# Lane numbering, the stored T and two split transfers in a recurrent-attention and expert kernel

## The chip, the cores and the metric

One core of one Trainium2 chip runs the whole program. The metric is device time in microseconds (us), of one execution of the program. Several executions of the kernel before were timed, and one was profiled.

## The reference, cut to what matters

All inputs are fp32 except the two dense weight matrices, which arrive as 64-bit floats and are converted on the chip. A recurrence over 768 steps runs for 4 batches of 8 heads with 40 x 40 states; its output, as 3072 tokens of 320 features, goes through a dense two-layer block (ELU between) and then through eight experts, chosen per token.

```python
# r, k, v, w, a, b: [4, 8, 768, 40]
for t in range(768):
    y[:, :, t] = einsum('bhd,bhde->bhe', rt, state)
    Sa = einsum('bhde,bhe->bhd', state, at)
    state = state * wt[:, :, None, :] - einsum('bhd,bhe->bhde', Sa, bt) + einsum('bhd,bhe->bhde', vt, kt)
x = y as [3072, 320]
h = x @ w_in                                   # [320, 2048]
x = where(h > 0, h, exp(min(h, 0)) - 1) @ w_out  # [2048, 320]
probs = softmax(x @ w_gate); e = argmax        # 8 experts
out[i] = probs[e] * (relu(x[i] @ w1[e]) @ w2[e])   # w1: 320 x 1024, w2: 1024 x 320
```

## The kernel before, in words

The 768 steps are cut into 24 chunks of 32 steps (C = 32). Two chunks make a pair (12 pairs), four chunks make a lane group (6 groups). There are 32 (batch, head) combinations.

**Lanes.** `lanes(g)` works on one group: 128 partitions, one for each of 4 chunks times 32 heads, each holding 32 steps x 40 features (1280 floats, 5 KB). It loads w, forms running products along the steps, multiplies a by them and stores the result to DRAM (`scr_A`), stores the products (`scr_W`), loads w again, forms the inverse products from the other end, multiplies b and k by those and stores both (`scr_BK`). Group 0 (the call with `room`) has its four loads and its stores on SP's DMA queue and its own tiles; groups 1 to 5 have five loads and four stores each on POOL's queue, in two tiles (`W`, `lx`) that are used again and again, and their arithmetic on POOL, in order with what else POOL does. Three places of a group wait on a load: L161 for w, L185 for the second w, L196 for k.

**Pairs.** `pre(p)` reads the scaled a, b, k by steps (`load_tok`: `tok` tiles, steps on partitions, 160-byte pieces), transposes them, multiplies, and masks the result into `TM`, whose T part goes to DRAM (`Td`, L290, two transfers per chunk). `inverse(p)` reads T back with one lane per partition (L306, twice, 64 lanes each), inverts 64 unit triangular 32 x 32 matrices on DVE by 31 rounds of about three instructions (L314, L319, L321), writes the result to DRAM (`Ud`, L325) and reads it back for each chunk as `UT` (L328). `chain(c)` is the recurrence proper for one chunk: products with `TM`, `UT` and the state `ST`, an evacuation times `Wp` at L448 near its end, and the loads of the next chunk's `Wp`, `BKd` and `pv`. `put` transposes the finished chunk for the dense block.

**Around it.** While the first chunks run, `Moe1.weights` converts the dense weights in 40 steps: a load on SP's queue into one of three `raw` buffers (L495), ACT (L499), DVE (L500 to L503), ACT (L472), and for the low part POOL (L473, L510). `Moe1.block(p)` is the dense block on the two chunks of pair p, `Router.tile(c)` then ranks the experts for one chunk, stores its 128 rows of 321 floats to DRAM (`rows`, L699, one transfer on SP) and scatters the token numbers (`list`). Then `Moe2` gathers rows by expert and runs the eight experts.

Generators are woven by step counts (`weave`), with priorities from `ahead`; the order of each engine's queue is then made by a planner that plays the program through with costs of its own (`schedule_with_timeline_sim=True`). Each engine and SP's queue run their instructions in that order, and an instruction that waits holds up all behind it on its engine.

```python
weave((ahead(tc, start(), 1000), 100), (conv, 60))   # start: lanes(0), pre(0), lanes(1), inverse(0), pre(1)
for p in range(NP + 1):
    ... chain(2p), chain(2p+1); lanes(p//2 + 2) over two p; inverse(p+1); pre(p+2); moe1.block(p-1)
```

Of the kernel before, what the change touches and what calls it, by code (L numbers as in the profile page):

```python
# [22 lines left out]
B, H, S, D = 4, 8, 768, 40  # L23
C = 32
NCH = S // C
NP = NCH // 2
# [7 lines left out]
ROW = DM + 1  # L34
# [4 lines left out]
class Attention:  # L39
# [7 lines left out]
    def __init__(self, ctx, tc, nc, r, k, v, w, a, b):  # L47
        self.nc, self.tc = nc, tc
        self.src = dict(r=r, k=k, v=v, w=w, a=a, b=b)

        def pool(name, **kw):
            return ctx.enter_context(tc.tile_pool(name=name, bufs=1, **kw))

        self.pers = pool("att", side="right")
        self.dr = pool("att_dram", space=DRAM)
        dr = lambda shape, name: self.dr.tile(shape, F32, name=name)
        self.scr_A = [dr([128, C, D], f"scr_A{g}") for g in range(NP // 2)]
        self.scr_W = [dr([128, C, D], f"scr_W{g}") for g in range(NP // 2)]
        self.scr_BK = [dr([128, 2 * C, D], f"scr_BK{g}") for g in range(NP // 2)]
        self.Td = [dr([C, 64, C], f"Td{p}") for p in range(NP)]  # L60
        self.Ud = [dr([C, 64, C], f"Ud{p}") for p in range(NP)]
        self.tiles = {}

# [62 lines left out]
    def lanes(self, g, eng, eng2=None, room=None):  # L126

        nc = self.nc
        eng2 = eng2 or eng
        W, la, wd = self.t("W"), self.t("lx"), self.t("WCd")
        V, lb, lk = room or (W, la, la)
        flat = lambda t: t.rearrange("p s d -> p (s d)")
        queue = nc.sync if room else nc.gpsimd

        def load(t, x):
            queue.dma_start(
                flat(t), self.src[x][:, :, 128 * g:128 * g + 128, :].rearrange("b h (c s) d -> c (b h) (s d)", c=4))  # L140

        def store(dst, t):
            for i in (0, 64) if room else (0,):
                q = slice(i, i + 64) if room else slice(0, 128)
                self.last = queue.dma_start(dst[q], t[q])

        w = V[:, 0:32, :] if room else W[:, 1:33, :]
        load(w, "w")
        load(la, "a")
        if room:  # L150
            load(lb, "b")
            load(lk, "k")
        nc.vector.memset(W[:, 0, :], 1.0)
        yield

        eight = lambda t: t.rearrange("p (q r) d -> p q r d", r=8)
        wq, Wq = eight(w), eight(W[:, 1:33, :])
        if room:
            eng.tensor_copy(Wq[:, :, 0], wq[:, :, 0])
        for r in range(1, 8):  # L160
            eng.tensor_tensor(Wq[:, :, r], Wq[:, :, r - 1], wq[:, :, r], ALU.mult)  # L161
            yield
        for q in range(1, 4):
            eng.tensor_tensor(
                Wq[:, q], Wq[:, q], W[:, 8 * q, :].unsqueeze(1).to_broadcast([128, 8, 40]), ALU.mult)
            yield
        nc.vector.tensor_copy(wd[:, 0:40], W[:, 32, :])
        nc.vector.tensor_copy(wd[:, 64:104], W[:, 32, :])
        nc.gpsimd.tensor_tensor(la, la, W[:, 0:32, :], ALU.mult)
        store(self.scr_A[g], la)  # L170
        if not room:
            store(self.scr_W[g], W[:, 0:32, :])
            load(W[:, 0:32, :], "w")
            load(lb, "b")
        ps = self.psum("p")
        nc.tensor.transpose(ps[0:104, 0:128], wd, self.ident)
        wt = self.t("WCT", g)
        v = ps[:, 0:128].rearrange("p (c i j) -> p c i j", c=4, j=2)
        nc.vector.tensor_copy(wt[0:40], v[0:40, :, :, 0])
        nc.vector.tensor_copy(wt[64:104], v[64:104, :, :, 1])  # L180
        yield
        nc.vector.reciprocal(V[:, 32, :], wd[:, 0:40])
        Vq = eight(V[:, 0:32, :])
        for r in range(6, -1, -1):
            eng.tensor_tensor(Vq[:, :, r], Vq[:, :, r + 1], Vq[:, :, r], ALU.mult)  # L185
            yield
        for q in range(3, -1, -1):
            eng.tensor_tensor(
                Vq[:, q], Vq[:, q], V[:, 8 * q + 8, :].unsqueeze(1).to_broadcast([128, 8, 40]), ALU.mult)
            yield  # L190
        eng2.tensor_tensor(lb, lb, V[:, 1:33, :], ALU.mult)
        store(self.scr_BK[g][:, 0:C], lb)
        if not room:
            load(lk, "k")
        yield
        nc.gpsimd.tensor_tensor(lk, lk, V[:, 1:33, :], ALU.mult)  # L196
        store(self.scr_BK[g][:, C:2 * C], lk)
        if room:
            for _ in range(2):
                self.load_tok()  # L200
            yield
            with self.tc.issue_after(self.last.ins):
                store(self.scr_W[g], W[:, 0:32, :])
        yield

    def load_heads(self, t, src, hg, s0, n):

        self.nc.sync.dma_start(
            t[:, :, 0:40], src[2 * hg:2 * hg + 2, :, s0:s0 + n, :].rearrange("b h s d -> s (b h) d"))

    def load_tok(self):

        if self.loaded == len(self.order):
            return
        kind, i = self.order[self.loaded]
        t = self.t("tok", self.loaded)
        self.loaded += 1
        for hg in range(2):
            rows = t[64 * hg:64 * hg + 64]
            if kind == "r":  # L220
                self.load_heads(rows, self.src["r"], hg, 64 * i, 64)
            elif kind == "a":
                for cc in range(2):
                    lane = (2 * (i % 2) + cc) * 32 + 16 * hg
                    self.nc.sync.dma_start(
                        rows[32 * cc:32 * cc + 32, :, 0:40],
                        self.scr_A[i // 2][lane:lane + 16].rearrange("l s d -> s l d"))
            else:
                lane = (i % 4) * 32 + 16 * hg
                self.last = self.nc.sync.dma_start(  # L230
                    rows[:, :, 0:40], self.scr_BK[i // 4][lane:lane + 16].rearrange("l x d -> x l d"))

    def turn(self, tag, evac):
        t = self.t("tok", self.taken)
# [25 lines left out]
    def pre(self, p):  # L260

        nc = self.nc
# [11 lines left out]
        for cc in range(2):  # L274
            c = 2 * p + cc
            ps = self.psum("p")
# [7 lines left out]
            TM = self.t("TM", c)  # L284
# [3 lines left out]
            )  # L288
            for hg in range(2):
                self.last = self.nc.sync.dma_start(  # L290
                    self.Td[p][:, 32 * cc + 16 * hg:32 * cc + 16 * hg + 16, :].rearrange("s l t -> s (l t)"),
                    TM[64 * hg:64 * hg + 32, :])
            if cc == 0:
                self.block_diagonal(Abd, AAT, 1, 'ss')
                yield
# [3 lines left out]
    def inverse(self, p):  # L299

        nc = self.nc
        TL, UL = self.t("TL"), self.t("UL")
        nc.vector.memset(UL, 0.0)
        for i in range(2):
            half = slice(64 * i, 64 * i + 64)
            self.last = self.nc.sync.dma_start(TL[half], self.Td[p].rearrange("s l t -> l s t"))  # L306
            nc.vector.memset(UL[half].rearrange("p a b -> p (a b)")[:, i::34], 1.0)
        yield
        for j in range(31):

            n, m = j // 2 + 1, 30 - j
# [13 lines left out]
            self.nc.sync.dma_start(  # L325
                self.Ud[p].rearrange("(a i) l t -> i l a t", i=2)[i], UL[64 * i:64 * i + 64])
        for cc in range(2):
            self.nc.sync.dma_start(  # L328
                self.t("UT", 2 * p + cc).rearrange("p h t -> p (h t)"),
                self.Ud[p][:, 32 * cc:32 * cc + 32, :].rearrange("s (b h) t -> b s (h t)", b=4))  # L330
        yield

    def load_pv(self, c):
# [2 lines left out]

    def load_bkd(self, c):
        for hg in range(2):
            lane = (c % 4) * 32 + 16 * hg
            self.nc.sync.dma_start(  # L340
                self.t("BKd", c)[64 * hg:64 * hg + 64], self.scr_BK[c // 4][lane:lane + 16].rearrange("l x d -> x l d"))

    def load_wp(self, c):
        for b in range(4):
            lane = (c % 4) * 32 + 8 * b
            self.nc.sync.dma_start(
                self.t("Wp")[32 * b:32 * b + 32].rearrange("p (h d) -> p h d", h=8),
                self.scr_W[c // 4][lane:lane + 8].rearrange("h s d -> s h d"))

    def bank(self, c):  # L350

# [265 lines left out]
class Router:  # L617
# [52 lines left out]
    def tile(self, c, o):  # L670
        nc, p = self.nc, self.p
        x2 = self.new_x2()
# [4 lines left out]
        s = lambda n, dt=F32, w=1: p.tile([128, w], dt, tag=n, name=n, bufs=1)  # L677
# [10 lines left out]
        ps = o[:, 400:512]  # L688
# [4 lines left out]
        at, place = s("at", w=E), s("place")  # L693
# [2 lines left out]
        nc.vector.tensor_reduce(place, at, AX.X, ALU.add)  # L696
        idx = p.tile([128, 1], I32, tag="idx", name="idx", bufs=2)
        self.last = nc.vector.tensor_copy(idx, place)  # L698
        nc.sync.dma_start(self.rows.rearrange("(b s) d -> b s d", b=B)[:, C * c:C * c + C, :], x2[:, 0:ROW])  # L699
        nc.gpsimd.indirect_dma_start(  # L700
            out=self.list[:, :], out_offset=bass.IndirectOffsetOnAxis(ap=idx.bitcast(U32)[:, 0:1], axis=0),
            in_=self.ids[:, c:c + 1], in_offset=None, bounds_check=E * LIST - 1, oob_is_err=False,
# [497 lines left out]
```

## Time and profile before

| what | value |
|---|---|
| timed runs of the kernel before | 1306.5, 1322.2, 1322.34 us; median 1322.2 us |
| the profiled execution | 1325.83 us |
| its span, first to last instruction | 1324.0 us, granted TensorE clock 0.927 of full |
| busy share of the span | PE 78%, DVE 61%, ACT 45%, POOL 23% |
| DMA | 325,645 packets, 131.27 MB, of which 292,808 packets are under 512 B |

The span is cut into 40 slices on the page; PE's busy share is low in the first ten and near 9 tenths from there on, while the DMA engines' mean busy share is highest in the first half. A mean over 16 DMA engines does not tell whether all of them are busy.

### The profile page before, as it was taken

Reading aid. Unit: us, or ns where it says so; the run is one execution under the profiler, and the core shown is the slowest. Engines: PE = TensorE matmul, PEld = TensorE weight load, DVE = VectorE, ACT = ScalarE, POOL = GpSimd, SP = SyncE. Lnnn points to the kernel's source line nnn. Section 1 sums busy time; section 2 is a strip of 40 time slices with the busy share of each in tenths; the row PEclk is TensorE's granted clock in tenths of the full one; section 3 lists DMA queues with packets and bytes.
Section 4 is the critical chain, followed back from the end, with each engine's and each line's share of the span. In section 5 each row is a group of like instructions: output and inputs, shape, how many; then the busy total and the mean of one; then the engine's idle time right before and its main releaser. Section 6 shows DMA issues by size and latency. Waiting matters only on the chain.

```text
span 1324.0 us, 35742 instructions
## 1 busy us (share of the span) xinstructions
PE 1037.8 (78%) x14568; PEld 945.8 (71%) x14568; DVE 802.2 (61%) x2714; ACT 598.3 (45%) x1498; POOL 299.6 (23%) x355
## 2 busy tenths in 40 slices
PE   0144165777769988989899999989989679999994
PEld 0133155666668777878788888889989679889994
DVE  2345675677448864878667686867555425655541
ACT  0233123445425544546455655656656425534430
POOL 4343253454231341021000000000000141232311
PEclk9999996898779988899899999989999879999997
DMA  3767456655563566455452536342130146545210
GB/s 99 167 157 134 114 128 135 139 154 107 134 141 68 112 125 132 68 100 104 68 88 45 90 56 101 53 81 49 28 89 11 35 116 174 138 127 162 76 41 19
DMA packets 325645, 131.27 MB, mean 99 GB/s; under 512 B 292808, under 2 KB 307280, under 8 KB 325472
## 3 DMA queue, kind: packets, MB, share of 16 engines
q1 hardware_dynamic: 304848, 89.24, 34.4%
q0 software_dynamic: 19664, 37.43, 10.1%
q8 instruction: 117, 1.92, 0.7%
q10 hardware_dynamic: 960, 2.23, 0.6%
q14 instruction: 56, 0.46, 0.1%
HBM read 99.13 MB, written 31.00 MB: 98 GB/s over the span
## 4 chain that ended last, share of the span: by engine, by line
DMA 27%; PE 24%; DVE 23%; issue 11%; ACT 3%; POOL 3%; SPq 2%; another core or an unknown queue 0%; ACTq 0%; POOLq 0%; DVEq 0%
DMA W<-in_w_dram 5%; PE ps_h L583 4%; DMA out_dram<-ys,ids 4%; DVE ut L314 3%; DVE inv L319 3%; DMA inv<-Td 3%; DVE inv L321 3%; PE ps_c L375 3%; DMA lx<-in_k_dram 2%; DMA raw<-in_moe_w_in_dram 2%; DMA Ud<-inv 2%; DVE ST L421 2%; PE ps_c L903 2%; PE ps_h L903 2%; DVE e L589 2%
## 5 line engine op out<-in xcount | busy, mean ns | idle before, releaser
L472 ACT CAST gH<-e 128x256 fp32r<-128x256 f32 x192 | 77.0, 405 | 136.0 <-DVE e L589 128.4
L597 PE MATMUL ps_o<-woH,gH 128*128 128x328 f32 x384 | 130.2, 341 | 9.6 <-ACT gH L472 9.6
L599 PE MATMUL ps_o<-woH,gL 128*128 128x328 f32 x384 | 120.7, 336 | 8.3 <-DVE gL L473 8.2
L598 PE MATMUL ps_o<-woL,gH 128*128 128x328 f32 x384 | 126.0, 330 | 0.0
L583 PE MATMUL ps_h<-xH,wiH 128*128 128x256 f32 x368 | 112.5, 307 | 13.4 <-DVE e L589 12.6
L700 POOL DMA_INDIRECT list<-ids,idx x24 | 24.6, 1026 | 429.9 <-DVE idx L698 322.0
L589 DVE SCALAR_TENSOR_TENSOR e<-e,ps_h 128x256 f32<-128x256 f32 x184 | 76.5, 417 | 60.5 <-ACT e L588 58.2
L314 DVE TENSOR_TENSOR ut<-inv 128x30 f32<-128x30 f32 (+4 forms) x360 | 95.1, 264 | 26.9 <-DMA inv<-Td 26.5
L583 PE MATMUL ps_h<-xL,wiH 128*128 128x256 f32 x368 | 109.7, 298 | 0.0
L583 PE MATMUL ps_h<-xH,wiL 128*128 128x256 f32 x368 | 109.0, 296 | 0.0
L473 DVE TENSOR_TENSOR gL<-e,gH 128x256 fp32r<-128x256 f32 x192 | 81.5, 429 | 30.2 <-ACT gH L472 26.8
L319 DVE SCALAR_TENSOR_TENSOR inv<-inv 128x1 f32<-128x1 f32 (+15 forms) x372 | 98.1, 264 | 0.5
L321 DVE TENSOR_TENSOR inv<-inv,ut 128x30 f32<-128x30 f32 (+4 forms) x360 | 96.0, 267 | 0.3
L587 ACT ACTIVATE e<-ps_h 128x256 f32<-128x256 f32 x184 | 70.7, 384 | 54.4 <-PE ps_h L583 35.2
L244 PE MATMUL ps_p<-ident,tok 128*104 128x128 f32 x288 | 55.5, 321 | 41.0 <-DMA tok<-scr_A 15.4
L583 PEld LDWEIGHTS ps_h<-xH,wiH 128*128 128x128 f32 x368 | 73.7, 201 | 18.7 <-DVE e L589 17.6
L597 PEld LDWEIGHTS ps_o<-woH,gH 128*128 128x128 f32 x384 | 77.6, 202 | 12.0 <-ACT gH L472 10.7
L599 PEld LDWEIGHTS ps_o<-woH,gL 128*128 128x128 f32 x384 | 73.8, 200 | 10.7 <-DVE gL L473 9.7
L588 ACT ACTIVATE e<-e 128x256 f32<-128x256 f32 x192 | 79.1, 416 | 4.1
L598 PEld LDWEIGHTS ps_o<-woL,gH 128*128 128x128 f32 x384 | 77.8, 203 | 0.2
L583 PEld LDWEIGHTS ps_h<-xL,wiH 128*128 128x128 f32 x368 | 74.6, 203 | 0.1
L583 PEld LDWEIGHTS ps_h<-xH,wiL 128*128 128x128 f32 x368 | 74.2, 202 | 0.0
(308 smaller groups left out, 2882.4 us busy)
## 6 DMA issues: line engine op xcount, KB each, us to landing
r<-in_moe_w_dram SPq DMA_DIRECT2D x15, 640.0 KB
tok<-scr_BK SPq DMA_DIRECT2D x48, 160.0 KB
BKd<-scr_BK SPq DMA_DIRECT2D x48, 160.0 KB
r<-in_moe_w_dram SPq DMA_DIRECT2D x7, 1024.0 KB
W<-in_w_dram POOLq DMA_DIRECT2D x10, 640.0 KB
scr_BK<-lx POOLq DMA_DIRECT2D x10, 640.0 KB
inv<-Td SPq DMA_DIRECT2D x24, 256.0 KB
raw<-in_moe_w_out_dram SPq DMA_DIRECT2D x16, 320.0 KB
```

Of the source, the lines that this page charges most:

```text
L314: nc.vector.tensor_tensor(tv, TL[:, j:j + 1, j + 2:32].to_broadcast([128, n, m]), UL[:, 0:n, j:j + 1].to_broadcast([128, n, m]), ALU.mult,)
L319: nc.vector.scalar_tensor_tensor(col, UL[:, 0:n, j], TL[:, j, j + 1:j + 2], col, ALU.mult, ALU.add)
L321: nc.vector.tensor_tensor(UL[:, 0:n, j + 2:32], UL[:, 0:n, j + 2:32], tv, ALU.add)
L472: split.last = nc.scalar.copy(H, x)
L473: return (low or nc.vector).tensor_tensor(L, x, H.bitcast(F32), ALU.subtract)
L583: nc.tensor.matmul(h, l, r, start=i == 0, stop=i == len(seq) - 1)
L587: nc.scalar.activation(e, h, AF.Relu, scale=-1.0)
L588: nc.scalar.activation(e, e, AF.Exp, scale=-1.0)
L589: nc.vector.scalar_tensor_tensor(e, e, -1.0, h, ALU.add, ALU.max)
L597: nc.tensor.matmul(o, gH[:, ts], self.woH[:, f], start=f == 0, stop=False)
L598: nc.tensor.matmul(o, gH[:, ts], self.woL[:, f], start=False, stop=False)
L599: nc.tensor.matmul(o, gL[:, ts], self.woH[:, f], start=False, stop=f == NF - 1)
```

## The change

Lanes are numbered head first: partition 4 x head + chunk instead of 32 x chunk + head. The load of L140 therefore lists the 32 heads before the 4 chunks on its DRAM side; the bytes are the same, 128 pieces of 5 KB. The DRAM copies of the lanes have the same order, and `of` picks the lanes of one chunk with a stride of four in the loads of `tok`, `BKd` and `Wp`, whose pieces stay as long as they were. The copy out of PSUM into `WCT` reads with a stride. T is stored lane by lane, `[64, 32, 32]`: its store now writes 32 x 16 pieces of 128 bytes in place of 32 pieces of 2 KB, and each of its two loads reads 64 pieces of 4 KB in place of 64 x 32 pieces of 128 bytes. The load of `UT` for a chunk becomes four transfers of 32 partitions (one per batch) in place of one whose outermost dimension is 4, and so does the store of `rows`.

```diff
-        self.Td = [dr([C, 64, C], f"Td{p}") for p in range(NP)]
+        self.Td = [dr([64, C, C], f"Td{p}") for p in range(NP)]
...
-                flat(t), self.src[x][:, :, 128 * g:128 * g + 128, :].rearrange("b h (c s) d -> c (b h) (s d)", c=4))
+                flat(t), self.src[x][:, :, 128 * g:128 * g + 128, :].rearrange("b h (c s) d -> (b h) c (s d)", c=4))
...
-        v = ps[:, 0:128].rearrange("p (c i j) -> p c i j", c=4, j=2)
+        v = ps[:, 0:128].rearrange("p (i j c) -> p c i j", c=4, j=2)
...
+    def of(self, t, c, first, n):
+
+        return t.rearrange("(l c) s d -> c l s d", c=4)[c, first:first + n]
...
-                    rows[:, :, 0:40], self.scr_BK[i // 4][lane:lane + 16].rearrange("l x d -> x l d"))
+                    rows[:, :, 0:40], self.of(self.scr_BK[i // 4], i % 4, 16 * hg, 16).rearrange("l x d -> x l d"))
...
-                    self.Td[p][:, 32 * cc + 16 * hg:32 * cc + 16 * hg + 16, :].rearrange("s l t -> s (l t)"),
-                    TM[64 * hg:64 * hg + 32, :])
+                    self.Td[p][32 * cc + 16 * hg:32 * cc + 16 * hg + 16].rearrange("l s t -> s l t"),
+                    TM[64 * hg:64 * hg + 32, :].rearrange("s (l t) -> s l t", t=C))
...
-            self.last = self.nc.sync.dma_start(TL[half], self.Td[p].rearrange("s l t -> l s t"))
+            self.last = self.nc.sync.dma_start(TL[half], self.Td[p])
...
         for cc in range(2):
-            self.nc.sync.dma_start(
-                self.t("UT", 2 * p + cc).rearrange("p h t -> p (h t)"),
-                self.Ud[p][:, 32 * cc:32 * cc + 32, :].rearrange("s (b h) t -> b s (h t)", b=4))
+            for b in range(4):
+                h = 32 * cc + 8 * b
+                self.returned = self.nc.sync.dma_start(
+                    self.t("UT", 2 * p + cc)[32 * b:32 * b + 32], self.Ud[p][:, h:h + 8, :])
...
-        nc.sync.dma_start(self.rows.rearrange("(b s) d -> b s d", b=B)[:, C * c:C * c + C, :], x2[:, 0:ROW])
+        for b in range(B):
+            at = S * b + C * c
+            nc.sync.dma_start(self.rows[at:at + C, :], x2[C * b:C * b + C, 0:ROW])
```

The loads of `tok` from `scr_A`, of `BKd` and of `Wp` take their lanes through `of` in the same way.

## Rows read from the trace of the kernel before

**Rows 1.** Busy time by engine in two stretches: clock, DMA share, GB/s last

```profile
core 0: us, PE busy (x) PEld busy (x) DVE busy (x) ACT busy (x) POOL busy (x), PEclk, DMA share, GB/s
0.00:400.00 400.00, 205.38 (x2954) 180.50 (x2954) 227.21 (x704) 131.15 (x343) 159.56 (x214) 0.89 0.60 134
400.00:971.00 571.00, 526.46 (x9781) 478.23 (x9776) 407.67 (x1584) 323.65 (x853) 58.69 (x61) 0.95 0.45 79
```

**Rows 2.** L448, once per chunk: ns min/median/max, first and last start

```profile
L448 DVE TENSOR_TENSOR xtok<-ps_c,Wp x5: 475/478/491, 200.6 to 398.7; 128x320 f32<-128x320 f32 x5
...
L448 DVE TENSOR_TENSOR xtok<-ps_c,Wp x18: 427/482/492, 200.6 to 970.7; 128x320 f32<-128x320 f32 x18
```

**Rows 3.** Chain of waits that ended last, 0 to 400 us, shares by line

```profile
by line: DMA W<-in_w_dram 15.6%; DMA lx<-in_k_dram 7.0%; DMA raw<-in_moe_w_in_dram 7.0%; DMA raw<-in_moe_w_out_dram 4.5%; issue 3.9%; DMA Ud<-inv 2.7%; DMA inv<-Td 2.6%; POOL W L161 2.6%; DVE ut L314 2.4%; DVE x L502 2.4%; SPq L230 2.0%; DV
```

**Rows 4.** Who waited for whom, 0 to 400 us: total us, times, longest

```profile
DVE x L500 <- ACT x L499: 75.1, 20, 12.8
ACT x L499 <- DMA raw<-in_moe_w_in_dram: 72.1, 11, 32.3
POOL W L185 <- DMA W<-in_w_dram: 53.2, 4, 16.0
...
POOL lx L196 <- DMA lx<-in_k_dram: 39.1, 3, 13.7
...
DVE inv L303 <- DMA Ud<-inv: 11.8, 2, 8.3
...
DVE W L159 <- DMA inv<-in_w_dram: 11.5, 1, 11.5
...
DVE ut L314 <- DMA inv<-Td: 9.8, 3, 4.7
```

**Rows 5.** POOL in order of time: start, us, instruction, [idle before and releaser]

```profile
331.84 0.60 POOL L145 DMA_DIRECT2D scr_BK<-lx  x1 [0.30 <-POOL lx L191]
335.40 0.70 POOL L139 DMA_DIRECT2D lx<-in_k_dram  x1 [2.96 <-DMA scr_BK<-lx]
348.20 2.87 POOL L196 TENSOR_TENSOR lx<-lx,W 128x1280 f32<-128x1280 f32 x1 [12.10 <-DMA lx<-in_k_dram]
```

**Rows 6.** SP's DMA issues in order of time, first 60 us

```profile
2.79 4.98 SPq L139 DMA_DIRECT2D keep<-in_k_dram  x1
7.82 7.25 SPq L632 DMA_DIRECT2D wg<-in_moe_w_gate_dram  x1
...
21.34 12.52 SPq L208 DMA_DIRECT2D pv<-in_v_dram  x4
...
51.15 8.17 SPq L230 DMA_DIRECT2D tok<-scr_BK  x2
```

**Rows 7.** Single pieces of the chain of waits: start, us, what

```profile
142.87 3.78 DMA raw<-in_moe_w_in_dram
...
208.19 17.05 DMA raw<-in_moe_w_in_dram
...
339.41 10.99 DMA Ud<-inv
...
374.25 10.51 DMA inv<-Td
...
566.65 3.90 DMA UT<-Ud
...
699.84 5.34 DMA inv<-Td
...
731.95 3.07 DMA Ud<-inv
...
879.00 1.71 DMA Td<-keep
```

**Rows 8.** Two lines' DMA issues on SP: ns min/median/max, first and last start

```profile
L290 SPq DMA_DIRECT2D Td<-keep x48: 312/418/6922, 82.0 to 879.0; - x48
...
L328 SPq DMA_DIRECT2D UT<-Ud x24: 530/554/695, 152.7 to 919.3; - x24
```

**Rows 9.** SP's own waits over the whole span: us, times, longest

```profile
SPq L699 <- DVE x L687: 87.5, 15, 34.6
```

More of the change, by code (lines that the diff above doesn't have):

```diff
@@ L223, in load_tok @@
                 for cc in range(2):
-                    lane = (2 * (i % 2) + cc) * 32 + 16 * hg
                     self.nc.sync.dma_start(
                         rows[32 * cc:32 * cc + 32, :, 0:40],
-                        self.scr_A[i // 2][lane:lane + 16].rearrange("l s d -> s l d"))
+                        self.of(self.scr_A[i // 2], 2 * (i % 2) + cc, 16 * hg, 16).rearrange("l s d -> s l d"))
             else:
-                lane = (i % 4) * 32 + 16 * hg
                 self.last = self.nc.sync.dma_start(
-                    rows[:, :, 0:40], self.scr_BK[i // 4][lane:lane + 16].rearrange("l x d -> x l d"))
+                    rows[:, :, 0:40], self.of(self.scr_BK[i // 4], i % 4, 16 * hg, 16).rearrange("l x d -> x l d"))
     def turn(self, tag, evac):
@@ L338, in load_bkd @@
         for hg in range(2):
-            lane = (c % 4) * 32 + 16 * hg
             self.nc.sync.dma_start(
-                self.t("BKd", c)[64 * hg:64 * hg + 64], self.scr_BK[c // 4][lane:lane + 16].rearrange("l x d -> x l d"))
+                self.t("BKd", c)[64 * hg:64 * hg + 64], self.of(self.scr_BK[c // 4], c % 4, 16 * hg, 16).rearrange("l x d -> x l d"))
     def load_wp(self, c):
         for b in range(4):
-            lane = (c % 4) * 32 + 8 * b
             self.nc.sync.dma_start(
                 self.t("Wp")[32 * b:32 * b + 32].rearrange("p (h d) -> p h d", h=8),
-                self.scr_W[c // 4][lane:lane + 8].rearrange("h s d -> s h d"))
+                self.of(self.scr_W[c // 4], c % 4, 8 * b, 8).rearrange("h s d -> s h d"))
     def bank(self, c):
```

## Prediction

> **What bounds the kernel now.** I read the view of busy time by stretch first, to see whether one limit holds for the whole span. It doesn't: up to 400 us PE is busy 205 of 400 us and DVE 227 [rows 1], while from 400 to 971 us PE is busy 526 of 571. The late stretch is near PE's own work; the early one waits. The line that ends each chunk says the same in chunks: five ends lie between 200.6 and 398.7 us, so the first four steps take 49.5 us each, and the other 19 chunks, up to 970.7 us, take 30.1 us each [rows 2]. Whatever shortens the early stretch moves all of the rest forward, since the rest is paced by PE's work and not by a clock time; whatever touches only the late stretch has to get past a busy PE.
>
> Then the chain of waits for the early stretch, to see what it consists of. Of 400 us, w loads of the lanes take 15.6% (62 us), k loads of the lanes 7.0% (28), the loads of the dense weights 7.0% and 4.5% (28 and 18), Ud 2.7% (11), the loads of T 2.6% (10), and issues of L230 2.0% (8): 166 us of transfers [rows 3]. The list of waits shows who stands still: POOL at L185 for 53.2 us and at L196 for 39.1, ACT at L499 for 72.1, and behind ACT the DVE at L500 for 75.1 [rows 4]. ACT and DVE are in the path of everything (conversion, chain, inverse share their queues), and POOL's lanes stand before POOL's part of the conversion, so a late lane load holds a `raw` buffer and through it the next conversion.
>
> Third, why those loads are slow. POOL's own timeline has a store and a load of the same size, 128 x 1280 floats, one after the other on the same queue: the store, issued at 331.84, has landed by 335.40 (3.6 us), the load issued at 335.40 has landed by 348.20 (12.8 us) [rows 5]. They differ in direction and in the order of dimensions: the load's DRAM side starts with the 4 chunks. A dense-weight load on the other queue took 3.78 us at 142.87, and 17.05 at 208.19 [rows 7], when POOL had just issued two lane loads; Ud took 10.99 us at 339.41, beside the k load of [rows 5], and 3.07 at 731.95, after the lanes had ended. So the slow loads slow the others too. At the start four lane loads stand on SP's queue, and behind them SP's issues stretch: 4.98 us for one, 7.25 us for the small `wg`, 12.52 for four of `pv` [rows 6].
>
> The Trainium skill's page "DMA: Bandwidth & Descriptors", section "Why a DMA increments its semaphore by 16 and not by 1", says that a transfer runs on the largest number of DMA engines, up to 16, that divides the slowest dimension of both sides. By it the load uses 4 engines now and 16 after the change, and the store 16 already, an estimate by the page of a quarter of the moving time; the 12.8 and 3.6 us agree, though no row shows which engines carry a transfer.
>
> **The change part by part.** Lane loads: 25 on POOL's queue and 4 on SP's. Each costs between 3.6 us (the store) and 12.8 (as now) [rows 5]; I take 5, near the store, because two are often under way together and other traffic is there too. So about 60% of a wait goes. For the transfers that run beside them the rows give 17.05 to 3.78 (78%) and 10.99 to 3.07 (72%) [rows 7]. I take two thirds of each wait on either kind.
>
> What this is worth on the path needs an engine that everything goes through. DVE's early waits that end with a transfer, directly or through ACT, are 75.1 + 11.8 + 11.5 + 9.8 = 108 us [rows 4]. Two thirds are 72 us. Two bounds: the chain's 166 us [rows 3] would give up 110, but the next-latest wait takes a part of that; and if only half of DVE's 72 is given back, because ACT, PE or POOL are late next, 36. After 72 us are gone DVE is busy 227 of 328 us, 69%, below the 71% that it has from 400 to 971 (408 of 571) [rows 1], so its own work doesn't forbid it; 110 gone would make it 78%.
>
> The start is inside these sums: DVE's first wait of 11.5 us, and ACT's longest, 32.3 us for the first weights [rows 4], which were issued behind the stretched issues of [rows 6].
>
> T: the loads go from 64 x 32 short pieces to 64 long ones, twice per pair. Undisturbed they take 5.34 us now; the floor is the 1.71 us that a T store of 32 long pieces takes, the ceiling no gain [rows 7]. I take 2.5, nearer to the floor since the pieces are longer yet: -2.8 per pair. The store becomes 512 pieces of 128 bytes. Between 1.71 (as now) and Ud's 3.07 (two transfers of 1024 such pieces each), I take 2.5: +0.8. Net -2.0 for each of 12 pairs, in a series (store, load, inverse) for which DVE waits only part of the time: in the late stretch PE's 92% [rows 1] covers most of it. I count -5, bounds 0 and -24, and the worst case is a rival below.
>
> The page's section "Specifications" wants at least 512 B per piece, below which a read-modify-write is done. By it the new T store would be the costly side; the 3.07 us of Ud, of such pieces, is the only measure here.
>
> UT: two issues at 0.55 us become eight; an issue of 32 partitions takes 0.42 [rows 8], so the last quarter of a chunk is issued 4 x 0.42 - 0.55 = 1.1 us later, and its landing, 3.90 us now [rows 7], may shrink to the 1.71 of a T store. Between -2.2 and +1.1 per pair; I take 0. Rows: one issue becomes four per chunk, and nothing before the experts reads them. Both together add 12 issues, 12 x 0.42 = 5.0 us of SP's queue per pair of 60 us. Queued behind are `load_tok`, `BKd`, `Wp`, `pv`. The cover is SP's idle time: it stood 87.5 us at the rows store alone, 15 times [rows 9]. So 0; uncovered it would be 5 us x 12 = 60.
>
> The strided lanes in `tok`, `BKd` and `Wp` keep pieces and counts: 0; so does the `WCT` copy, 12 in the kernel, each smaller than the 0.48 us evacuations of [rows 2].
>
> Sum against the profiled execution: 1325.8 - 72 - 5 = 1249. It was 3.6 us over the median of 1322.2, so 1245 for the forecast.
>
> **The rivals.** *The chain gives all*: two thirds of its 166 us and the T gain, 110 + 5 and a few us for the start (the chain view begins at 43 us): about 1322 - 125 = 1197. For it speaks that each late wait is the same congestion; against it that waits overlap, and DVE at 78%. *Half*: in-order queues replace each removed wait with the next (ACT's for PE, POOL's for ACT are in the same list); 1322 - 36 = 1286. *The loads don't spread*: direction, not order, made 12.8 out of 3.6; then only T's -5 is left, 1317. Against it stands that a load on SP's queue took 3.78 [rows 7]. *T's store becomes the wait* (slower): at L290, before each load of T. If 512-piece stores take what Ud took in its worst row, 10.99 instead of 1.71, the net is +9.3 - 2.8 = +6.5 per pair, 78 us over 12 pairs; with only the half gain of 36 that is 1322 + 42 = 1364. It decides from 5.2 us net per pair (36 + 26 over 12). Against it: 10.99 stood beside a lane load, and those shorten. The planner may also order queues anew; that has no row, and the width takes it in.
>
> **How the numbers follow.** Forecast 0.60 (its own range 1215 to 1280); all of the chain 0.10; half 0.17 (1272 to 1305); no spreading 0.09; slower 0.04. A measurement of this kernel tells about 2% (26 us) from no change. Faster by more than that: 0.60 + 0.10 + 0.14 of the half case = 0.84; within: 0.03 + 0.09 = 0.12; slower 0.04. For 8 in 10 the range takes the forecast's, most of the half case and the upper part of the chain's: 1200 to 1295.
>
> **What would show it.** The k load of [rows 5] in about 5 us, the weight loads all near 4, SP's first issues below 1 us, the first L448 near 150 us instead of 200.6, the fifth near 325, and 30 us per chunk after that. T's load below 3 us on the chain. The prediction fails if L448's spacing in the early stretch stays near 50 us though the lane loads are short (another engine's work was the limit), or if the late spacing rises.

## The result

The changed kernel takes 1229.3 us (median of four runs, 1227.4 to 1238.5) against 1322.3 for the kernel before: a ratio of 0.9333, 95% interval 0.9245 to 0.9421, some 88 us less. The ratio is taken over all undisturbed runs and is not the quotient of the two medians, which lie 93.0 us apart. The forecast was 1245, range 1200 to 1295. The profiled execution took 1227.4 us with a span of 1225.7, against 1325.8 and 1324.0.

Where the time came from is seen by cutting both spans at the same events: the start of the fifth chunk's evacuation (398.7 before [rows 2], 310.7 after) and of the last one's (970.7, 882.5). Busy time by engine in the three stretches, first of the kernel before, then of the changed one; columns as in [rows 1]:

```profile
0.00:398.70 398.70, 204.58 (x2940) 179.94 (x2940) 225.91 (x700) 130.77 (x341) 158.42 (x212) 0.89 0.60 134
398.70:970.70 572.00, 526.97 (x9794) 478.49 (x9788) 408.70 (x1587) 324.03 (x854) 59.83 (x63) 0.95 0.45 79
970.70:1324.00 353.30, 306.27 (x1841) 287.36 (x1841) 167.62 (x428) 143.54 (x303) 81.38 (x81) 0.92 0.32 93
```

```profile
0.00:310.70 310.70, 190.56 (x2938) 164.93 (x2939) 235.63 (x704) 129.87 (x338) 158.80 (x216) 0.86 0.70 171
310.70:882.50 571.80, 525.93 (x9792) 475.06 (x9792) 412.48 (x1585) 325.15 (x857) 55.03 (x58) 0.96 0.42 79
882.50:1225.70 343.20, 307.76 (x1841) 287.87 (x1841) 167.63 (x428) 142.48 (x303) 79.73 (x81) 0.93 0.33 95
```

Each engine does nearly the same number of instructions in a stretch as before. The first stretch is 88.0 us shorter, the second 0.2, the third 10.1. DVE's busy time in the first even grew by 9.7 us, for a reason that no run here shows; its idle time fell from 172.8 to 75.1. The third stretch is what follows the recurrence, the experts above all. It takes 341.0 to 357.2 us in the 14 profiles on record, and 351.2 in a second profile of the same changed kernel (run e4 below), so the 10 us are scatter of single executions. Of the other two stretches e4 tells how far they hold: its first is 83.8 us shorter than before, its second 8.0 longer.

L449 is the chunk's evacuation in the changed kernel's numbering; 57.1 of the 88 us are won before the first chunk's evacuation, the other 30.9 in the four steps up to the fifth (41.8 us each, 49.5 before). Rows as in [rows 2], the second for the fifth chunk alone:

```profile
L449 DVE TENSOR_TENSOR xtok<-ps_c,Wp x18: 478/484/493, 143.5 to 882.5; 128x320 f32<-128x320 f32 x18
...
L449 DVE TENSOR_TENSOR xtok<-ps_c,Wp x1: 484/484/484, 310.7 to 310.7; 128x320 f32<-128x320 f32 x1
```

The waits of that stretch, 0 to 310.7 us of the changed kernel, answer to [rows 4]:

```profile
DVE x L501 <- ACT x L500: 22.8, 12, 5.1
...
DVE ut L316 <- DMA inv<-Td: 8.2, 2, 6.6
...
DVE W L159 <- DMA inv<-in_w_dram: 4.1, 1, 4.1
...
DVE inv L305 <- DMA Ud<-inv: 2.5, 1, 2.5
...
POOL lx L196 <- DMA lx<-in_k_dram: 7.2, 3, 4.4
...
POOL W L185 <- DMA W<-in_w_dram: 3.4, 1, 3.4
...
ACT x L500 <- DMA raw<-in_moe_w_in_dram: 26.2, 13, 9.5
```

POOL's waits for the second w and for k fell to a ninth (92.3 to 10.6 us), ACT's for the first weight matrix from 72.1 to 26.2, DVE's behind ACT from 75.1 to 22.8. The k load that took 12.8 us in [rows 5] takes 4.9 (issued at 246.63, used at 251.56), by POOL's timeline:

```profile
246.63 0.55 POOL L139 DMA_DIRECT2D lx<-in_k_dram  x1 [4.34 <-DMA scr_BK<-lx]
251.56 2.93 POOL L196 TENSOR_TENSOR lx<-lx,W 128x1280 f32<-128x1280 f32 x1 [4.38 <-DMA lx<-in_k_dram]
```

The five k loads on that queue, each from its issue to the multiplication that waits for it, took 12.1 to 14.4 us in the kernel before (median 12.8) and take 4.3 to 7.0 in the changed one (median 5.3).

The transfers beside them are shorter too. Pieces of the changed kernel's chain of waits, to be read against [rows 7]:

```profile
105.61 5.85 DMA Ud<-inv
...
117.32 4.06 DMA raw<-in_moe_w_in_dram
...
147.73 4.37 DMA raw<-in_moe_w_in_dram
...
158.80 3.84 DMA Ud<-inv
```

The loads of the second weight matrix still take up to 8.1 us on that chain (17.9 before), and no lane load is among its longer pieces.

SP's issues behind the first lane loads no longer stretch, as they did in [rows 6]; only `pv` still does, four issues in 4.77 us. SP's queue in order of time:

```profile
2.83 0.60 SPq L139 DMA_DIRECT2D keep<-in_k_dram  x1
3.48 0.59 SPq L633 DMA_DIRECT2D wg<-in_moe_w_gate_dram  x1
...
6.25 4.77 SPq L208 DMA_DIRECT2D pv<-in_v_dram  x4
```

That the loads are spread is visible directly. In the first microseconds lane loads alone are under way before the change. Two stretches of 2 us of the kernel before (the last two columns are the mean busy share of the 16 DMA engines and GB/s), and the same of the changed kernel, where later transfers are already issued, but by their sizes the packets under way are still those of the lane loads (a share above 1 means that recorded times of packets overlap):

```profile
4.00:6.00 2.00, 0.00 (x0) 0.00 (x0) 0.00 (x0) 0.00 (x0) 1.87 (x3) 1.00 0.25 77
6.00:8.00 2.00, 0.00 (x0) 0.00 (x0) 0.00 (x0) 0.00 (x0) 2.00 (x4) 1.00 0.24 64
```

```profile
4.00:6.00 2.00, 0.00 (x0) 0.00 (x0) 0.84 (x3) 0.00 (x0) 1.87 (x3) 1.00 1.06 407
6.00:8.00 2.00, 0.00 (x0) 0.00 (x0) 1.83 (x7) 0.00 (x0) 2.00 (x4) 1.00 0.96 366
```

A mean share of 0.25 can be 4 engines all the time or 16 a quarter of the time. The trace's list of packets (the pieces that are moved, each with its start and length) tells more: between 4 and 6 us exactly 4 packets are under way for 1.63 of the 2.00 us in the kernel before, and exactly 16 for 1.48 in the changed one. With four loads queued only 4 pieces move at a time; on which engines, no row shows. That is the count that the Trainium skill's page "DMA: Bandwidth & Descriptors" (section "Why a DMA increments its semaphore by 16 and not by 1") gives for an outermost dimension of 4, and the trace agrees with it.

### The profile page after: what moved, and what is told of

It reads as the page before. It is cut to its first block, busy times and chain, and to the rows that moved or that the text cites. A ratio compares the mean times of both kernels' runs of the same rounds, so it can differ in the third digit from the quotient of the medians.

```text
span 1225.7 us, 35923 instructions
## 1 busy us (share of the span) xinstructions
PE 1024.3 (84%) x14568; PEld 927.9 (76%) x14568; DVE 815.7 (67%) x2714; ACT 597.5 (49%) x1498; POOL 293.6 (24%) x355
## 4 chain that ended last, share of the span: by engine, by line
PE 30%; DVE 25%; DMA 24%; issue 8%; ACT 5%; SPq 4%; POOL 2%; POOLq 0%; DVEq 0%; ACTq 0%
PE ps_h L584 8%; DMA out_dram<-ys,ids 6%; PE ps_c L376 4%; DVE ut L316 4%; DVE inv L323 3%; DVE inv L321 3%; DMA inv<-Td 3%; PE ps_o L598 3%; PE ps_o L600 3%; PE ps_o L599 3%; DMA Td<-keep 2%; DMA Ud<-inv 2%; DVE ST L422 2%; DVE e L590 2%; DVE gL L474 2%
## 5 line engine op out<-in xcount | busy, mean ns | idle before, releaser
L584 PE MATMUL ps_h<-xH,wiH 128*128 128x256 f32 x368 | 113.0, 308 | 18.7 <-DVE e L590 17.9
L316 DVE TENSOR_TENSOR ut<-inv 128x30 f32<-128x30 f32 (+4 forms) x360 | 102.1, 284 | 29.9 <-DMA inv<-Td 29.6
L474 DVE TENSOR_TENSOR gL<-e,gH 128x256 fp32r<-128x256 f32 x192 | 89.7, 471 | 31.7 <-ACT gH L473 23.2
L584 PE MATMUL ps_h<-xH,wiL 128*128 128x256 f32 x368 | 108.2, 294 | 0.0
L588 ACT ACTIVATE e<-ps_h 128x256 f32<-128x256 f32 x184 | 70.5, 384 | 49.5 <-PE ps_h L584 33.3
L321 DVE SCALAR_TENSOR_TENSOR inv<-inv 128x1 f32<-128x1 f32 (+15 forms) x372 | 93.7, 252 | 0.5
```

Of the source, the lines that this page charges most:

```text
L316: nc.vector.tensor_tensor(tv, TL[:, j:j + 1, j + 2:32].to_broadcast([128, n, m]), UL[:, 0:n, j:j + 1].to_broadcast([128, n, m]), ALU.mult,)
L321: nc.vector.scalar_tensor_tensor(col, UL[:, 0:n, j], TL[:, j, j + 1:j + 2], col, ALU.mult, ALU.add)
L474: return (low or nc.vector).tensor_tensor(L, x, H.bitcast(F32), ALU.subtract)
L584: nc.tensor.matmul(h, l, r, start=i == 0, stop=i == len(seq) - 1)
L588: nc.scalar.activation(e, h, AF.Relu, scale=-1.0)
```

## The experiments

The theory: the outermost dimension of the lane loads is the whole gain; T, UT and rows are worth nothing here. Rivals: it is the head-first order itself; or T and the split transfers carry part. All times are against the kernel before on the same chip.

**e1, the lanes alone.** From the changed kernel, T, UT and rows are put back:

```diff
-        self.Td = [dr([64, C, C], f"Td{p}") for p in range(NP)]
+        self.Td = [dr([C, 64, C], f"Td{p}") for p in range(NP)]
...
-            for b in range(4):
...
+            self.nc.sync.dma_start(
+                self.t("UT", 2 * p + cc).rearrange("p h t -> p (h t)"),
+                self.Ud[p][:, 32 * cc:32 * cc + 32, :].rearrange("s (b h) t -> b s (h t)", b=4))
...
-        for b in range(B):
...
+        nc.sync.dma_start(self.rows.rearrange("(b s) d -> b s d", b=B)[:, C * c:C * c + C, :], x2[:, 0:ROW])
```

> The lanes numbered head first and nothing else: T stored by steps, UT and rows each in one transfer. If the spreading of the lane loads is the whole gain: 0.93 to 0.945 of the kernel before, the fifth L449 near 310 us. If the T layout and the split transfers carry a third or more of it: 0.96 or above. If the split UT and rows transfers or the short T stores cost time in the changed kernel, this one is under it, below 0.925.

Measured: 0.9432 (0.9395 to 0.9469), 1247.5 us; the fifth L448 at 323.5 us. That is 75 us, six sevenths of the gain. It lies at the top of the range for "the whole gain", yet its interval doesn't meet that of the changed kernel timed beside it (e4 below), so a last seventh comes from elsewhere.

**e2, everything but the lanes.**

```diff
-                flat(t), self.src[x][:, :, 128 * g:128 * g + 128, :].rearrange("b h (c s) d -> (b h) c (s d)", c=4))
+                flat(t), self.src[x][:, :, 128 * g:128 * g + 128, :].rearrange("b h (c s) d -> c (b h) (s d)", c=4))
...
-        return t.rearrange("(l c) s d -> c l s d", c=4)[c, first:first + n]
+        return t.rearrange("(c l) s d -> c l s d", c=4)[c, first:first + n]
```

> The changed kernel with the lanes numbered as before (load with the 4 chunks outermost): only T, UT and rows are changed. If the lanes are the whole gain: 0.99 to 1.01 of the kernel before, five chunk ends still some 50 us apart. If the rest has a gain of its own: below 0.98. If the 12 added issues per pair and the short stores hurt where SP's queue is held up: above 1.02.

Measured: 1.0160 (1.0114 to 1.0207), 1343.0 us, between two of the ranges. The lanes are not the whole story in the other sense: without them the rest of the change loses 21 us. So the parts don't add up. The loss lies behind the early stretch: the fifth chunk's evacuation is at 394.6 us, no later than before (398.7), and the last at 989.6 instead of 970.7.

**e3, the change without T; e4, the change again.** e3 puts back the T lines of e1's diff alone.

> The changed kernel with T stored by steps again (2 KB store pieces, 128-byte load pieces). By my step T is worth 5 us, so 0.937 of the kernel before, unclear from the changed kernel. If the short stores cost what the chain of the changed kernel shows at Td (pieces of 3.7 to 6.9 us where the kernel before had 1.7 to 5.7): 0.92 to 0.93.

> The changed kernel itself, on the same chip as the other three: 0.925 to 0.942 of the kernel before. It says how far two timings of one kernel lie apart.

Measured: 0.9319 (0.9258 to 0.9380) without T, 0.9337 (0.9297 to 0.9377) with it. T is worth nothing that can be told in the changed kernel: by these two it costs 2 us, and the intervals leave room for some 10 either way. Two timings of the changed kernel agree. Between e1 and e3 only UT and rows differ, and those intervals don't meet: on spread lane loads the two together are worth some 15 us.

**e5, the old numbering, four transfers per load.** The lanes are numbered as before; each load is cut so that the 32 heads are outermost:

```diff
-            queue.dma_start(
-                flat(t), self.src[x][:, :, 128 * g:128 * g + 128, :].rearrange("b h (c s) d -> (b h) c (s d)", c=4))
+            src = self.src[x][:, :, 128 * g:128 * g + 128, :].rearrange("b h (c s) d -> c (b h) (s d)", c=4)
+            for c in range(4):
+                queue.dma_start(flat(t)[32 * c:32 * c + 32], src[c])
```

> The changed kernel with the lanes numbered as before, each lane load cut into four transfers, one per chunk, so that each has the 32 heads outermost: 29 loads become 116 transfers. If the outermost dimension of a transfer is what made the loads slow: near the changed kernel, 0.93 to 0.95, the k load of a group landing in 4 to 6 us. If it is the head-first numbering itself (the order in which DRAM is read): as the kernel without the lanes, 1.00 to 1.02.

Measured: 0.9305 (0.9246 to 0.9363), 1229.2 us. Not the numbering, then: with the old one the time is the changed kernel's, and the 87 added transfers cost nothing that shows in it. The k loads themselves took 5.3 to 9.1 us from the first of their four issues, longer than the 4 to 6 expected.

**e6, an outermost dimension of 8.**

```diff
+            heads = self.src[x].rearrange("b h s d -> (b h) s d")
+            queue.dma_start(
+                flat(t), heads.rearrange("(n m) s d -> m n s d", m=4)[0, :, 0:512, :].rearrange("n (c s) d -> n c (s d)", c=16))
```

> The changed kernel with lane loads of one transfer each whose outermost dimension is 8: they read 16 chunks of every fourth head in place of 4 chunks of every head, so the numbers are others, pieces and bytes the same. If the spreading goes by the outermost dimension: lane loads of 6 to 8 us, a DMA share near one half while only they run at the start, and a time between, 0.95 to 0.98. If any outermost dimension but 4 does: as the changed kernel, 0.93 to 0.94.

The lane loads of this kernel read the first 16 chunks of every fourth head, the same for each group, and leave the other heads out. The tokens may go to other experts by that; its last stretch takes 343.7 us, within the range above.

Measured: 0.9681 (0.9631 to 0.9732), 1279.9 us: between. The k load that corresponds to the one above, issued at 287.30, is used at 294.87, so 7.6 us against 12.8 and 4.9, and the DMA share at the start lies between as well (POOL's timeline, then a stretch of 2 us, both of e6):

```profile
287.30 0.61 POOL L140 DMA_DIRECT2D lx<-in_k_dram  x1 [2.96 <-DMA scr_BK<-lx]
294.87 2.91 POOL L197 TENSOR_TENSOR lx<-lx,W 128x1280 f32<-128x1280 f32 x1 [6.96 <-DMA lx<-in_k_dram]
```

```profile
4.00:6.00 2.00, 0.00 (x0) 0.00 (x0) 0.00 (x0) 0.00 (x0) 1.87 (x3) 1.00 0.55 151
```

In that stretch exactly 8 packets are under way for 1.51 of the 2.00 us. Over the five k loads, outermost 4, 8 and 32 give 12.1 to 14.4, 7.6 to 9.6 and 4.3 to 7.0 us; from the first to the last 5 KB packet of each, 9.7 to 12.0, 5.5 to 7.3 and 2.5 to 4.4 us. With the rest of the change in place the ratios are 1.016, 0.968 and 0.933. So the number of pieces that move at a time, and with it the length of the load, follows the outermost dimension.

**e7 and e8: which part loses without the lanes.** e7 is the kernel before with UT and rows split, e8 with T by lanes.

> The kernel before with only UT and rows in four transfers each. The kernel without the lanes lost 1.6%. If the 12 added issues per pair on SP's queue are the cause: 1.01 to 1.02. If T's short stores are: 0.99 to 1.00, and the next run has the loss.

> The kernel before with only T stored by lanes. If the store of 512 short pieces beside slow lane loads is what lost 1.6% without the lanes: 1.01 to 1.02, with DVE waiting longer for T in the late stretch (31 us there, 17 in the kernel before). If T is worth the 5 us that I gave it: 0.99 to 1.00.

Measured: 1.0279 (1.0217 to 1.0341) for the splits, more than either expectation had, and 1.0098 (1.0049 to 1.0147) for T. Both lose on the kernel before, the splits more; together (e2) they lost 1.6%, not the sum. They lose in different places: e7's fifth evacuation lies at 433.4 us (398.7 before), e8's at 396.3. In e8 DVE waited 41.7 us for T's loads over the span, 31.9 of that behind the fifth evacuation; in the kernel before it was 26.5 and 16.7:

```profile
DVE ut L316 <- DMA inv<-Td: 41.7, 9, 8.2
```

**e9 and e10: UT alone, rows alone, on the kernel before.** e9 has UT's four transfers of the front diff, e10 those of rows.

> The kernel before with only UT in four transfers. UT and rows split together lost 2.8% there. If UT is the part that loses (its transfers, spread over all DMA engines, wait behind the slow lane loads, and T's load is queued behind them on SP): 1.02 to 1.03, DVE's wait for T far over the 27 us of the kernel before. If both lose by their issues alone, six per pair each: 1.01 to 1.015 in both runs.

> The kernel before with only rows in four transfers. If rows are the part that loses: 1.02 to 1.03. If UT is: 0.995 to 1.005. My step had 0 for it.

Measured: 1.0270 (1.0181 to 1.0360) for UT, 1.0009 (0.9957 to 1.0061) for rows. UT is the part that loses. Its fifth evacuation lies at 429.2 us instead of 398.7, and nearly all of that is lost in one step, from the third evacuation to the fourth: 68.4 us, 41.5 in the kernel before. The two evacuations, and the waits of e9 between them:

```profile
L449 DVE TENSOR_TENSOR xtok<-ps_c,Wp x2: 476/484/492, 306.0 to 374.4; 128x320 f32<-128x320 f32 x2
```

```profile
ACT x L500 <- DMA raw<-in_moe_w_in_dram: 15.6, 1, 15.6
...
DVE x L501 <- ACT x L500: 14.7, 1, 14.7
...
DVE inv L305 <- DMA Ud<-inv: 9.5, 1, 9.5
```

Nothing in that step waits for UT, and no issue of UT stands on SP's queue in it before 373.54. A load of the dense weights stands behind four `Wp` loads whose issues take 8.5 us, beside two lane loads of POOL (issued at 305.98 and 313.01), and DVE waits for it behind ACT. e9's SP queue:

```profile
307.40 8.51 SPq L347 DMA_DIRECT2D Wp<-scr_W  x4
316.02 2.39 SPq L496 DMA_DIRECT2D raw<-in_moe_w_in_dram  x3
...
373.54 0.77 SPq L332 DMA_DIRECT2D UT<-Ud  x2
```

e7 loses in the same step (66.6 us, with a wait of 15.4 for the weights). e2, which has T by lanes besides, makes the same eight UT issues per pair beside the same slow lane loads and loses nothing up to the fifth evacuation; there the eight stand together on SP's queue:

```profile
362.50 7.40 SPq L332 DMA_DIRECT2D UT<-Ud  x8
```

So four transfers for one need not lose beside slow lane loads. What goes with the loss is another order of the queues around them; that the order alone makes it is not shown, since a kernel with the order held fixed wasn't tried.

**e11 and e12: the same two on top of the lanes.**

> Lanes head first and UT in four transfers, T and rows as before. The lanes alone gave 0.943, lanes with UT and rows 0.932. If UT carries that difference: 0.930 to 0.935. If rows do: 0.940 to 0.946, as the lanes alone.

> Lanes head first and rows in four transfers, T and UT as before. If rows carry the difference between 0.943 and 0.932: 0.930 to 0.935. If UT does: 0.940 to 0.946. If the difference is no more than the scatter between builds and chips, both of the last two lie between.

Measured: 0.9364 (0.9270 to 0.9458) with UT, 0.9413 (0.9334 to 0.9492) with rows, against 0.9432 for the lanes alone and 0.9319 with both (e3). UT leans towards the gain and rows towards none, but the intervals of e11 and e12 overlap both of the others; which of the two carries the last 1%, and whether by its transfers or by a new order of the queues, stays open. No run beat the changed kernel clearly.

## Why the prediction was right, step by step

*Which stretch.* Right: the early stretch gave all, the late one 0.2 us of 572, as PE's 92% there had said. The first evacuation came at 143.5 us (forecast near 150), the fifth at 310.7 (near 325), and the late steps stayed at 30.1 us.

*The lane loads, 5 us each.* Right: 4.3 to 7.0, and POOL's longest waits for w and k in the stretch are 3.4 and 4.4. The direction (load or store) isn't the reason: e5 and e6 change loads alone, and the time follows their outermost dimension. *The loads don't spread* is refuted by the shares 0.25, 0.55 and 1.06.

*Two thirds of each DVE wait, 72 us.* The size was right, in part by luck. The lanes alone (e1) give 75 us, and their early stretch is 75.2 us shorter. The four waits that I summed fell there from 108.2 [rows 4] to 44.2 us, by 64.0. Busy time of e1 up to the fifth evacuation, and the four waits in it:

```profile
0.00:323.50 323.50, 207.86 (x2998) 180.18 (x2999) 243.72 (x727) 134.07 (x353) 158.46 (x216) 0.84 0.69 165
```

```profile
DVE x L500 <- ACT x L499: 18.9, 13, 3.7
...
DVE ut L316 <- DMA inv<-Td: 14.2, 3, 6.5
...
DVE inv L305 <- DMA Ud<-inv: 6.7, 2, 3.6
...
DVE W L159 <- DMA inv<-in_w_dram: 4.4, 1, 4.4
```

DVE's other idle time, which I had left out, fell by 29.0, and its busy time in the stretch rose by 17.8 (727 instructions for 700): 64.0 + 29.0 - 17.8 = 75.2. The waits on PE fell by 17.8 and those on POOL by 13.1. The latter are these two behind POOL's lanes in the kernel before, which I had not followed to the transfers behind them:

```profile
DVE W L153 <- POOL W L188: 8.0, 1, 8.0
...
DVE WCd L167 <- POOL W L164: 5.1, 1, 5.1
```

In the changed kernel, whose four waits are shown in the section on the result, the same sum is 70.6 + 27.1 - 9.7 = 88.0. The bound from DVE's load was right: it is busy 235.6 of 310.7 us now, 76%. *The chain gives all* (110 and more) and *half* (36) lie on both sides, as they should.

*T, -5 us.* Not found: e3 and e4 tell no gain, though they can't rule out 5 us. The row that I took for a floor was wrong. 1.71 us is a store of 64 KB; T's load moves two times 256 KB, and on the changed kernel's chain it takes 3.8 to 5.5 us where I had 2.5 (5.3 to 10.5 before, so the 5.34 that I started from was the lowest). The store takes 2.0 to 6.9, before 1.7 to 5.7:

```profile
283.23 6.88 DMA Td<-keep
...
431.41 2.00 DMA Td<-keep
...
434.01 4.32 DMA inv<-Td
...
787.82 4.87 DMA Td<-keep
...
793.28 4.37 DMA inv<-Td
```

What the load wins, the store can lose. *T's store becomes the wait*: with the slow lane loads in place the T layout does lose (e8, +13 us), and DVE's wait for T's loads is 15.2 us longer; how much of that the store before the load makes is not shown. On spread lane loads (e3 and e4) no such loss can be told.

*UT and rows, 0.* This is the term that the forecast had wrong: on spread lane loads the two together give some 15 us (e1 and e3), and that makes up the distance between the 77 us that were forecast and the 88 measured: 75 for the lanes, 15 for UT and rows, nothing told for T. On the kernel before, rows alone are 0 (e10) and UT alone costs 36 us (e9). I named SP's idle time as the cover, from the 87.5 us in which it stood at the rows store [rows 9]; neither result goes by it. In e9 the lost time doesn't stand at UT's issues at all. That the planner may order the queues anew, which I had left to the width of the range, fits both, but no run shows that it is the cause.

## What to carry to other kernels

Read the DMA share in a stretch in which one kind of transfer runs alone: a quarter there, with a mean of 0.6 elsewhere, was here a load of which 4 pieces moved at a time in place of 16, and the transfers beside it were longer too. Before a wait is priced, follow every wait on another engine to the transfer behind it: the four waits that name a transfer gave 64 of the 93 us of idle time that the lanes took away. Measure the parts of a change on top of the main one as well as alone: UT split by itself loses 2.7%, and on spread lane loads it doesn't. And when an edit that looks free costs time, look for the step in which it is lost before you blame the edited line.

## What the runs showed of the hardware

A load on POOL's queue whose outermost dimension is small carries more packets than its bytes need. Packets, MB and share of POOL's queue in the kernel before (outermost 4), in e6 (8) and in the changed kernel (32), one row of each page:

```profile
q0 software_dynamic: 19664, 37.43, 10.1%
```

```profile
q0 software_dynamic: 13264, 37.41, 11.3%
```

```profile
q0 software_dynamic: 10064, 37.39, 9.3%
```

The bytes are the same to 0.1%. Over the 25 lane loads on that queue the differences are 9600 / 25 = 384 and 3200 / 25 = 128 packets per load above those of the spread one. All of them are packets of 4 bytes: in the trace every k load has 128 packets of 5 KB, and beside these 400, 144 and 16 of 4 bytes for outermost 4, 8 and 32. e5, with four transfers for each load, has 11264 packets on that queue, 16 more for each of its 75 added transfers. What the 4-byte packets do no run here shows.

Two profiles of one and the same changed kernel differ by 20 us of span (1225.7 and, in e4, 1246.1, granted clock 0.926 and 0.911), 4 of them in the first stretch and 8 in each of the others; a difference of 10 us between single profiles says nothing about an edit.
